# Two products of the last pair of tiles but one are moved into the last pair's order, and one more output goes out whole from ScalarE

## The chip, the cores and the metric

The kernel runs on one core of a Trainium2 chip. The metric is the device time of one execution in microseconds (us). A core has TensorE (matrix products, results in PSUM), VectorE, ScalarE, GpSimd and SyncE, each with its own queue of instructions that it takes in order, and 16 DMA engines that move data between HBM and SBUF. In the profile they are called PE (PEld for its weight loads), DVE, ACT, POOL and SP; a name with a q (SPq, ACTq) is the queue's own work, such as issuing a DMA.

## What is computed

Attention over 8 batches, 12 heads, 448 tokens and 64 columns a head, and behind it a two-layer network on the 3584 tokens with 768 columns, with 2048 columns between the layers:

```python
def _attn_ref(q, k, v):
    scores = np.matmul(q, k.transpose(0, 1, 3, 2)) / np.sqrt(q.shape[-1])
    attn = np.exp(scores - np.max(scores, axis=-1, keepdims=True))
    attn = attn / (np.sum(attn, axis=-1, keepdims=True) + 1e-09)
    return np.matmul(attn, v)

def _moe_ref(x, w_in, w_out):
    h = x @ w_in
    g = h * (1.0 / (1.0 + np.exp(-h)))
    return g @ w_out
```

The change touches the last product alone, `g @ w_out`, at its very end.

## The kernel before, in words

**Tiles and stages.** Scores, exponentials and attention come first, unit by unit; the first layer follows for two batches at a time, and the second layer, `g @ w_out`, mixes in as its inputs come free. In the last 40 us only the second layer runs. Its rows are cut into 28 tiles of 128 tokens, and two neighbouring tiles make a pair, numbered 0 to 13 (`qd` in the code; `LAST` is 13). Each of the two tiles has two halves of 384 output columns, so a pair has four output blocks of 128 x 384, called (0,0), (0,1), (1,0) and (1,1): tile, half.

**Seven products for eight.** A pair computes its four blocks with seven block products in place of eight, in Winograd's manner: each product runs over eight 128-row pieces, so it is eight matmuls of 128 x 384 (L922, L683 within `times`). Products 1, 2, 4 and 7 take rows of G (the activated first layer), products 5, 6 and 3 take rows S that VectorE combines from G beforehand (`combine_g`, L916). Three buffers S exist (`NSG`, L273). On the side of the weights, products 1, 2, 3 and 7 use `w_out_t` and 4, 5 and 6 combined weights D. So the profile's tile names tell the products apart: `w_out_t,G` is 1, 2 or 7, `D,S` is 5 or 6, and `w_out_t,S` is 3.

**Banks and reads.** Products 1, 6, 7 (and 4) add up in one PSUM bank, 5 and 3 in a second, 2 stands alone in a third (`BANK`, L918). Four banks are handed round. After product 1 ScalarE copies the bank to block (0,0), after 5 to (1,1), after 6 to (0,1) (`take_copy`, L1004). Product 6 may begin only when the copy of 1 is done, 7 only when the copy of 6 is done, 3 only when the copy of 5 is done, since each adds to what the copy reads. After 2, 7 and 3 VectorE adds the bank to (0,0), (1,1) and (0,1) and the block is stored (`take_sum`, L1023). In pairs 12 and 13 product 4 is itself replaced by a smaller scheme of seven products over both pairs, run ahead of pair 12 (`FOLD`, `AHEAD_OF`); the block (1,0) is completed and stored after product 7 by `take_last` (L1018). In pair 13, the last, product 2 is cut into two halves of 192 columns that stand at the very end; each is added and stored by `take_end` (L1010, its DMAs in L1014).

**Stores.** `store` (L981, DMA in L997) cuts a block by the batch in which its rows lie: rows of batches other than the last go out in pieces of 32, rows of the last batch in 64 or 128. In pairs 12 and 13 the pieces go in turn to SyncE and ScalarE. Pair 13's block (1,0) goes out whole, from ScalarE (L989, L995); its blocks (1,1) and (0,1) go out as two halves of 64 rows each, one from SyncE and one from ScalarE.

**What sets the order.** The program's order is written out by a planner inside the kernel (`Order`, and the loop at its end). It keeps a list `moe` of pieces of TensorE work with their inputs, and whenever TensorE is free it runs the first piece of the list whose inputs are ready and whose bank is free (`moe_ready`, L1876, over the first 80 pieces); pieces are single matmuls of a product (L1832). `queue_quad` (L1738) puts a pair's products into the list: for pairs before the last in the order 1, 5, 6, 2, 7, 3, 4, for the last 1, 5, 6, 7, 3, 4 and then the two halves of 2 (L1826). The reads and stores of a product are written out by the planner when the product is due to end. The engines then take their queues in order.

Of the kernel before, what the change touches and what calls it, by code (L numbers as in the profile page):

```python
# [29 lines left out]
def mm(n):  # L30
    return n / 2400.0 + 0.0026
# [183 lines left out]
def kernel(  # L215
# [42 lines left out]
    folded = {(q, m) for a, b, ms in FOLD for q in (a, b) for m in ms}  # L258
# [15 lines left out]
    LAST = NT * B // 4 - 1  # L274
# [447 lines left out]
    HF = NFF // 2  # L722
# [199 lines left out]
    def product(qd, m, f0, f1, strips, c0=0, c1=OH):  # L922
        w = {1: rows(2 * qd, 0), 2: rows(2 * qd, 1), 4: rows(2 * qd + 1, 1), 7: rows(2 * qd + 1, 0)}
        w = w[m] if m in w else S_t[(qd, m)]
        if BANK[m] == m and f0 == 0:
            pr_t[(qd, m)] = psum_bank(f"p_{qd}_{m}" + "r" * (c0 > 0))
        if c1 - c0 < OH:
            half_t[c0] = pr_t[(qd, m)]
        for f in range(f0, f1):
            times(  # L930
                pr_t[(qd, BANK[m])][:, 0 : c1 - c0],
                w[:, f, :],
                W_[m][:, f, c0:c1],
                f == 0 and BANK[m] == m,
                f == HF - 1,
                strips,
            )
# [43 lines left out]
    def store(qd, i, j):  # L981
        u, t = divmod(2 * qd + i, NT)
        w, turn = 0, 0
        while w < 4:
            r, col = divmod(128 * t + 32 * w, S)
            b = 2 * u + r
            dst = out[b * S : (b + 1) * S, OH * j : OH * (j + 1)]
            if b == B - 1:
                n = 4 if w == 0 and (qd < LAST or (i, j) == OUT[4]) else 2  # L989
                dst = dst[col : col + 32 * n]  # L990
            else:
                n = 1
                dst = dst.rearrange("(i g) m -> g i m", g=TPP)[col // 32]
            eng = nc.scalar if turn % 2 and 4 * qd + 8 >= NT * B else nc.sync
            if qd == LAST and (i, j) == OUT[4]:  # L995
                eng = nc.scalar
            eng.dma_start(out=dst, in_=ost_t[(qd, i, j)][32 * w : 32 * (w + n), :])  # L997
            w, turn = w + n, turn + 1

    OUT = {1: (0, 0), 5: (1, 1), 6: (0, 1), 4: (1, 0)}  # L1000
    SUM = {2: (0, 0), 7: (1, 1), 3: (0, 1)}
# [6 lines left out]
    def take_end(p, c0, c1):  # L1008
        t = ost_t[(LAST, 0, 0)][:, c0:c1]
        nc.vector.tensor_tensor(out=t, in0=p, in1=t, op=ALU.add)  # L1010
        row = out.shape[0] - 256
        for lo, eng in ((0, nc.sync), (64, nc.scalar)) if c0 else ((0, nc.sync),):
            hi = lo + 64 if c0 else 128
            eng.dma_start(out=out[row + lo : row + hi, c0:c1], in_=t[lo:hi])  # L1014
# [222 lines left out]
    def take_bank(name):  # L1237
        bank_of[name] = m_ring.take()

    def leave_bank(name):  # L1240
        return lambda at: m_ring.give(at, bank_of[name])
# [336 lines left out]
    def sum_read(qd, m, at):  # L1578
        made = sum_reads.setdefault((qd, m), [])
        made.append(at)  # L1580
        if m and len(made) == (1 if m == 3 else 3):
            sg_ring.give(max(made))
# [40 lines left out]
    def plan_folds():  # L1623
# [24 lines left out]
        for i in (1, 2, 3, 4):  # L1648
# [2 lines left out]
                Op("DVE", 0.43, lambda i=i: fold_x(g, m, i, homes[i - 1]), made + more, 1)  # L1651
            )

    fold_done, ahead, ends = [], {}, []

    def queue_fold(g, m):
# [81 lines left out]
    def queue_quad(qd):  # L1738
# [4 lines left out]
        def read(m, deps):  # L1743
            def then(at):
                if m in (2, 3, 4):
                    leave_bank(f"p_{qd}_{BANK[m]}")(at)
                if m in (2, 3, 4, 7) and (qd, m) not in folded:
                    home.give(at + STORE)

            fn, eng = (take_copy, "ACT") if m in OUT else (take_sum, "DVE")  # L1750
            busy = act(OH) if eng == "ACT" else OH / 960.0 + 0.13
            bias = -2 if eng == "ACT" else -4
            took[m] = od.add(Op(eng, busy, lambda: fn(qd, m), deps, bias, then=then))

        def queue(m, f0, f1, c0=0, c1=OH):
            first = {6: (1,), 2: (1,), 7: (6, 5), 3: (5, 6) if qd == LAST else (5, 6, 7), 4: (7,)}.get(m, ())

            def run():
                strips = od.mode == "cols" and bool(qk_seq or av_seq)
                op = Op(  # L1760
                    "PE",
                    (f1 - f0) * mm(c1 - c0),
                    lambda: product(qd, m, f0, f1, strips, c0, c1),
                    tail=PE_OUT,
                )
                if BANK[m] == m and f0 == 0:
                    take_bank(f"p_{qd}_{m}" + "r" * (c0 > 0))
                for ring, need in rings:
                    ring.take(need)
                if m in (5, 6, 3) and f1 == HF:  # L1770
                    op.then = lambda at: sum_read(qd, m, at)
                od.on_pe(op, "cols" if strips else "full", (f1 - f0) * (4 if strips else 1))
                if f1 < HF or c1 < OH:
                    begun[m] = (HF if c0 else 0) + f1
                if f1 < HF:
                    return
                if c1 - c0 < OH:
                    fn = lambda: take_end(half_t[c0][:, 0 : c1 - c0], c0, c1)
                    od.add(Op("DVE", 0.33, fn, [op, took[1]], -4))
                    return  # L1780
                pr_op[(qd, m)] = op
                read(m, [op] + [took[x] for x in {2: (1,), 7: (5,), 3: (6,)}.get(m, ())])
                if m == 7 and (qd, 4) in folded:
                    if qd in ahead:
                        def then(at):
                            leave_bank(f"p_{qd}_1")(at)
                            home.give(at + STORE)

                        od.add(
                            Op(  # L1790
                                "DVE",
                                OH / 960.0 + 0.13,
                                lambda: take_last(qd),
                                [op, took[7], ahead[qd]],
                                -4,
                                then=then,
                            )
                        )
                    else:
                        read(4, [op, took[7]])  # L1800

            def deps():
                if f0 or c0:
                    return [] if begun.get(m) == (HF if c0 else 0) + f0 else [None]
                made = list(w_op.get(m, [None]))
                hard = {6: (1,), 7: (6,), 3: (5,), 4: (7,)}.get(m, ())
                made += [took.get(x) if x in hard else (took.get(x), 9.0) for x in first]
                if m in (1, 2, 4):
                    t = 2 * qd + m // 4
                    i = int(m != 1)  # L1810
                    for f in range(HF):
                        made += [(y, f * mm(OH)) for y in gates_at(t, f + HF * i)]
                    return made + ld_wout
                x = sg_op.get((qd, m), [None, None])
                return made + [x[0], (x[1], 4 * mm(OH))]

            rings = ((home, 1),) if f0 == 0 and (m in OUT or m == 7 and (qd, 4) in folded and qd not in ahead) else ()
            moe.append((deps, int(BANK[m] == m and f0 == 0), run, rings))


        begun = {}
        took_of[qd] = took
        for g, k in AHEAD_OF:
            if min(FOLD[g][:2]) - LEAD == qd:
                queue_fold(g, k)
        for m in (1, 5, 6, 2, 7, 3, 4) if qd < LAST else (1, 5, 6, 7, 3, 4):  # L1826
            if m == (3 if TAIL and qd == LAST else 4):
                for g, (a, b, ms) in enumerate(FOLD):
                    for k in ms if max(a, b) == qd else ():
                        if (g, k) not in AHEAD_OF:  # L1830
                            queue_fold(g, k)
            for f0 in range(0, HF, 1):  # L1832
                if (qd, m) not in folded:
                    queue(m, f0, f0 + 1)
        if qd == LAST and TAIL:
            ends.pop()()
        elif qd == LAST:
            for c in range(2):
                for f0 in range(0, HF, 1):
                    queue(2, f0, f0 + 1, OH // 2 * c, OH // 2 * (c + 1))  # L1840
# [347 lines left out]
    while True:  # L2188
# [45 lines left out]
        m = m_ring.when(1)  # L2234
        dark = m is None or m > od.now
        if warm["on"] and not dark and od.free["PE"] <= od.now and wait > QUIET and od.now > 0.9:
            each = mm(128) if od.now > COLD else 0.107
            n = max(1, int((wait - 0.06) / each), int(wait / each + 0.9) * (od.now < COLD))
            wide = 4
            if warm.pop("first", None):  # L2240
                n, wide = FIRST, 4
# [36 lines left out]
```

## Time and profile before

| | |
|---|---|
| time, median of 3 runs | 380.45 us (380.25 to 380.97) |
| the profiled execution | 379.91 us |
| its span in the profile | 378.1 us |
| granted TensorE clock | 0.999 |
| VectorE, ScalarE, GpSimd busy | 75%, 68%, 22% of the span |
| read from HBM, written | 45.61 MB, 11.01 MB |

The span runs from the first to the last instruction that the profiler saw; the execution's own time has 1.8 us more around it. A row of the timeline gives start, duration, engine, line, operation, tiles, shapes and count; what stands in brackets is the idle time before it and what ended that. A matmul's end is modelled and lies past the start of the next one, since matmuls overlap. A row for a DMA on SPq or ACTq is the time that the queue takes to issue it; its data move later, and the landing is told in the view of the DMAs. A row of the windows gives the stretch and its length, then busy time and count for PE, PEld, DVE, ACT and POOL, the granted clock, the DMA share and GB/s.

### The profile page before, as it was taken

The page shows a single profiled execution, that of the slowest core. Times are in us where ns is not written, and L with a number is a line of the kernel's source. Part 1 is how long each engine was busy: PE and PEld are TensorE (multiplying, and loading weights), DVE is VectorE, ACT ScalarE, POOL GpSimd, SP SyncE. Part 2 cuts the span into 40 slices and gives each one's busy share as a digit, 9 for nine tenths or more (in the row PEclk, how much of TensorE's full clock was granted, in tenths as well). Part 3 has the DMA queues.
Part 4 walks back from the last instruction along what each step waited for, and adds up shares of the span by engine and source line. Part 5 has one row for each costly group of instructions (what it writes and reads, how often), then busy time and mean ns, then how long its engine had stood idle before and what let it go on. Part 6 is the DMA issues. An engine that isn't in the chain of part 4 may idle for free.

```text
span 378.1 us, 9953 instructions
## 1 busy us (share of the span) xinstructions
PE 371.4 (98%) x4018; PEld 187.4 (50%) x4018; DVE 284.0 (75%) x588; ACT 255.7 (68%) x401; POOL 85.0 (22%) x155
## 2 busy tenths in 40 slices
PE   8999999999999999999999999999999999999994
PEld 3365445444544444444444444445556655556763
DVE  3667959999995969995969998897575334489852
ACT  4988873897877797868788778558872248873210
POOL 6652438433026316006423200000000000000000
PEclk9999999999999999999999999999999999999999
DMA  7999999928149849048955421200002330001343
GB/s 118 199 207 210 207 203 177 195 29 121 19 101 152 146 50 138 12 105 114 179 67 74 53 53 33 69 17 0 2 2 68 85 96 5 0 0 44 85 127 83
DMA packets 35982, 34.47 MB, mean 91 GB/s; under 512 B 11872, under 2 KB 35168, under 8 KB 35936
## 3 DMA queue, kind: packets, MB, share of 16 engines
q0 software_dynamic: 25312, 22.82, 40.7%
q1 hardware_dynamic: 10144, 10.48, 10.3%
q8 instruction: 31, 0.51, 0.5%
q10 hardware_dynamic: 480, 0.54, 0.4%
q14 instruction: 15, 0.12, 0.1%
HBM read 45.61 MB, written 11.01 MB: 150 GB/s over the span
## 4 chain that ended last, share of the span: by engine, by line
PE 96%; DMA 1%; ACT 1%; DVE 1%; issue 0%; DVEq 0%; POOLq 0%
PE p L683 29%; PE h L683 21%; PE f L683 16%; PE s L446 12%; PE a L568 8%; PE o L683 3%; PE a L554 2%; PE a L601 2%; PE n_Q L683 1%; DMA rk<-in_k_dram 1%; PE n_P L683 1%; ACT T L491 1%; PE z L2180 0%; PE z L683 0%; DVE ost L1023 0%
## 5 line engine op out<-in xcount | busy, mean ns | idle before, releaser
L502 ACT ACTIVATE E<-s 128x896 f16<-128x896 f32 x164 | 141.9, 922 | 24.7 <-PE s L446 24.6
L683 PE MATMUL h<-xT,w_in_t 128*32 128x448 f16 (+2 forms) x762 | 83.6, 348 | 0.0
L683 PEld LDWEIGHTS <-w_in_t 128*128 128x128 f16 (+1 forms) x909 | 54.5, 97 | 50.1 <-issue 8.1
L352 POOL DMA_DIRECT2D V<-in_v_dram x88 | 48.4, 561 | 48.8 <-PE a L568 29.2
L683 PEld LDWEIGHTS <-G 128*128 128x128 f16 (+1 forms) x672 | 42.5, 97 | 29.7 <-issue 5.0
L715 ACT ACTIVATE th<-h 128x448 f16<-128x448 f32 x67 | 36.6, 546 | 24.2 <-PE h L683 21.0
L683 PE MATMUL p<-w_out_t,G 128*128 128x384 f16 (+2 forms) x326 | 50.9, 324 | 0.0
L446 PE MATMUL s<-rq,KT 32*128 32x448 f16 (+3 forms) x728 | 45.4, 347 | 0.6 <-DVE rq L410 0.3
L1004 ACT COPY ost<-p 128x384 f32<-128x384 f32 x42 | 20.1, 480 | 31.8 <-PE p L683 20.6
L683 PEld LDWEIGHTS <-S 128*128 128x128 f16 (+1 forms) x321 | 29.5, 98 | 22.1 <-issue 3.4
L759 DVE SCALAR_TENSOR_TENSOR G<-th,h 128x448 f16<-128x448 f16 (+1 forms) x64 | 35.7, 573 | 4.7 <-ACT th L715 4.3
L683 PE MATMUL p<-D,S 128*128 128x384 f16 (+1 forms) x217 | 38.8, 326 | 0.0
L1023 DVE TENSOR_TENSOR ost<-p,ost 128x384 f32<-128x384 f32 x31 | 17.1, 552 | 23.7 <-ACT ost L1004 12.6
L568 PE MATMUL a<-E,V 128*32 128x448 f16 (+1 forms) x640 | 32.7, 356 | 0.0
L332 POOL DMA_DIRECT2D rq<-in_q_dram x25 | 14.0, 560 | 68.9 <-PE s L446 59.8
L671 DVE SCALAR_TENSOR_TENSOR xT<-a,rdn 128x448 f16<-128x448 f32 x46 | 26.9, 618 | 2.9 <-PE a L568 2.2
L446 PEld LDWEIGHTS <-KT 32*128 32x128 f16 (+1 forms) x824 | 12.5, 96 | 31.0 <-issue 29.7
L515 DVE TENSOR_TENSOR T<-T,E 128x1792 f16<-128x1792 f16 x21 | 22.8, 1086 | 4.5 <-ACT E L502 4.4
L515 DVE TENSOR_TENSOR T<-E,E 128x1792 f16<-128x1792 f16 x21 | 22.7, 1083 | 4.1 <-ACT E L502 4.0
L886 DVE TENSOR_TENSOR p<-f,p 128x448 f32<-128x448 f32 x15 | 9.3, 623 | 19.2 <-PE f L683 11.5
L683 PE MATMUL f<-sx,tw 128*128 128x448 f16 x102 | 23.4, 352 | 0.0
L568 PEld LDWEIGHTS <-V 128*32 128x32 f16 (+1 forms) x640 | 13.5, 95 | 18.1 <-issue 10.5
(128 smaller groups left out, 455.9 us busy)
## 6 DMA issues: line engine op xcount, KB each, us to landing
out_dram<-ost SPq DMA_DIRECT2D x163, 48.0 KB, 1.8
rk<-in_k_dram POOLq DMA_DIRECT2D x24, 224.0 KB, 5.5
rq<-in_q_dram POOLq DMA_DIRECT2D x23, 224.0 KB, 5.8
w_out_t<-in_moe_w_out_dram POOLq DMA_DIRECT2D x4, 768.0 KB, 12.5
V<-in_v_dram POOLq DMA_DIRECT2D x42, 64.0 KB, 4.3
V<-in_v_dram POOLq DMA_DIRECT2D x42, 48.0 KB, 4.7
w_in_t<-in_moe_w_in_dram POOLq DMA_DIRECT2D x6, 256.0 KB, 9.3
w_in_t<-in_moe_w_in_dram POOLq DMA_DIRECT2D x3, 512.0 KB, 12.0
```

The lines of the kernel that those rows point to most:

```text
L332: nc.gpsimd.dma_start(out=rawq[n][:, cols], in_=group_of(q, b, hg)[:, cols])
L352: nc.gpsimd.dma_start(out=VT[b][32 * x : 32 * (x + 1), hs, at : at + count, :], in_=v[b, hs].rearrange("h (i g) d -> i h g d", g=TPP)[:, : ...
L446: nc.tensor.matmul(out=pS[p0 : p0 + 32 * (x1 - x0), h % 2, at : at + q1 - q0], lhsT=KT[(b, hg)][32 * h : 32 * (h + 1), key_rows(b, hg, c, ...
L502: nc.scalar.activation(out=E[(n, w)][:, 2 * y : 2 * y + 2, :], in_=pS_t[(n, w, y)][:, :, 0:S], func=AF.Exp, scale=attn_scale,)
L515: nc.vector.tensor_tensor(out=T[n], in0=T[n] if step else E[(n, 0)], in1=E[(n, step + 1)], op=ALU.add,)
L568: nc.tensor.matmul(out=a[32 * h : 32 * (h + 1), 0:S], lhsT=VT[b][k0:k1, HG * hg + h, place(b, hg, c), part - 1 :: 2], rhs=e[k0:k1, h], sta ...
L671: nc.vector.scalar_tensor_tensor(out=x3(b, cc)[:, cc % 3, 32 * g0 : 32 * g1], in0=acc[(n, part)][:, 0:nq], scalar=0.5, in1=rdn_t[n].rearra ...
L683: nc.tensor.matmul(out=out[i : i + cut], lhsT=w[:, i : i + cut], rhs=x, start=start, stop=stop, skip_group_check=True,)
L715: nc.scalar.activation(out=th, in_=h_t[(b, f, t0)][:, 0:n], func=AF.Tanh)
L759: nc.vector.scalar_tensor_tensor(out=dst[:, f, at + lo : at + hi], in0=th_t[(b, f, t0)][:, lo - t0 : hi - t0], scalar=1.0, in1=h_t[(b, f, ...
L1004: nc.scalar.copy(out=ost(qd, *OUT[m]), in_=bank(qd, BANK[m]))
L1023: nc.vector.tensor_tensor(out=t, in0=bank(qd, BANK[m]), in1=t, op=ALU.add)
```

## The change

Pair 12 no longer puts its products 3 and 2 into the list. It leaves its `queue` function in `kept`, and pair 13 calls it: all eight matmuls of 12's product 3 stand behind 13's product 6, and all eight of 12's product 2 behind 13's product 7. The list is then 1, 5, 6, 7 for pair 12, and for pair 13: 1, 5, 6, (12's 3), 7, (12's 2), 3, and the two halves of 2. What each product computes, reads and stores stays as it is. Besides, pair 13's block (0,1), `SUM[3]`, is stored as one DMA of 128 rows from ScalarE in place of 64 rows from SyncE and 64 from ScalarE.

```diff
@@ -986,13 +986,13 @@
             b = 2 * u + r
             dst = out[b * S : (b + 1) * S, OH * j : OH * (j + 1)]
             if b == B - 1:
-                n = 4 if w == 0 and (qd < LAST or (i, j) == OUT[4]) else 2
+                n = 4 if w == 0 and (qd < LAST or (i, j) in (OUT[4], SUM[3])) else 2
                 dst = dst[col : col + 32 * n]
             else:
                 n = 1
                 dst = dst.rearrange("(i g) m -> g i m", g=TPP)[col // 32]
             eng = nc.scalar if turn % 2 and 4 * qd + 8 >= NT * B else nc.sync
-            if qd == LAST and (i, j) == OUT[4]:
+            if qd == LAST and (i, j) in (OUT[4], SUM[3]):
                 eng = nc.scalar
             eng.dma_start(out=dst, in_=ost_t[(qd, i, j)][32 * w : 32 * (w + n), :])
             w, turn = w + n, turn + 1
@@ -1651,6 +1651,7 @@
+    kept = []
     fold_done, ahead, ends = [], {}, []
...
@@ -1819,6 +1820,7 @@
         begun = {}
+        left_over, kept[:] = (kept or [None])[0], [queue]
         took_of[qd] = took
...
@@ -1830,8 +1832,11 @@
             for f0 in range(0, HF, 1):
-                if (qd, m) not in folded:
+                if (qd, m) not in folded and not (qd == LAST - 1 and m in (3, 2)):
                     queue(m, f0, f0 + 1)
+            for k, at in ((3, 6), (2, 7)) if qd == LAST else ():
+                for f0 in range(0, HF * (m == at), 1):
+                    left_over(k, f0, f0 + 1)
```

## The prediction

> **What bounds the kernel now.** I read the page first: which engine is busy, and which chain ended last.
>
> ```profile
> span 378.1 us, 9953 instructions
> PE 371.4 (98%) x4018; PEld 187.4 (50%) x4018; DVE 284.0 (75%) x588; ACT 255.7 (68%) x401; POOL 85.0 (22%) x155
> PE 96%; DMA 1%; ACT 1%; DVE 1%; issue 0%; DVEq 0%; POOLq 0%
> ```
>
> TensorE is busy for 98% of the span and is 96% of the chain that ended last. The change takes no matmul away and adds none, so it can gain only where TensorE waits, or after its last matmul. Next, TensorE's timeline from the place where the moved products stand. Columns: start, duration, line, tiles, count.
>
> ```profile
> 361.11 3.09 PE L683 MATMUL p<-w_out_t,G 128*128 128x384 f16 x18
> 364.04 1.46 PE L683 MATMUL p<-w_out_t,S 128*128 128x384 f16 x8
> 365.34 1.14 PE L683 MATMUL p<-w_out_t,G 128*128 128x384 f16 x6
> 366.31 2.76 PE L683 MATMUL p<-D,S 128*128 128x384 f16 x16
> 368.91 0.41 PE L683 MATMUL p<-w_out_t,G 128*128 128x192 f16 x3
> 369.16 0.81 PE L683 MATMUL p<-w_out_t,S 128*128 128x384 f16 x4
> 369.81 1.46 PE L683 MATMUL p<-w_out_t,G 128*128 128x384 f16 x8
> 371.11 0.81 PE L683 MATMUL p<-w_out_t,S 128*128 128x384 f16 x4
> 371.76 0.58 PE L683 MATMUL p<-w_out_t,G 128*128 128x192 f16 x5
> 372.17 0.82 PE L683 MATMUL p_2r<-w_out_t,G 128*128 128x192 f16 x8
> ```
>
> I write 12.2 for product 2 of pair 12. By the operands, the 18 are 12.2, 12.7 and two of 13.1; then come 12.3, the other six of 13.1, 13.5 and 13.6, three of 13.2's first half, half of 13.3, 13.7, the rest of 13.3, and 13.2. From 364.04 to 365.34 eight matmuls take 1.30 us, 0.1625 each, and every row starts where the one before leaves off: TensorE waits nowhere. Its last matmul ends at 372.17 + 0.82 = 372.99. The span ends at 378.1, so 5.1 us lie behind it. VectorE's and the DMA issues' timelines show what fills them:
>
> ```profile
> 371.38 0.56 DVE L1023 TENSOR_TENSOR ost<-p,ost 128x384 f32<-128x384 f32 x1 [4.56 <-PE p L683]
> 371.86 0.55 DVE L1018 TENSOR_TENSOR ost<-p,ost 128x384 f32<-128x384 f32 x1
> 372.32 0.55 DVE L1023 TENSOR_TENSOR ost<-p,ost 128x384 f32<-128x384 f32 x1
> 372.78 0.35 DVE L1010 TENSOR_TENSOR ost<-p,ost 128x192 f32<-128x192 f32 x1
> 373.05 0.34 DVE L1010 TENSOR_TENSOR ost<-p_2r,ost 128x192 f32<-128x192 f32 x1
> ```
>
> ```profile
> 371.97 0.47 SPq L997 DMA_DIRECT2D out_dram<-ost  x1
> 371.97 0.54 ACTq L997 DMA_DIRECT2D out_dram<-ost  x1
> 372.60 0.76 ACTq L997 DMA_DIRECT2D out_dram<-ost  x1
> 372.89 0.47 SPq L997 DMA_DIRECT2D out_dram<-ost  x1
> 373.46 0.65 ACTq L997 DMA_DIRECT2D out_dram<-ost  x1
> 373.46 0.54 SPq L1014 DMA_DIRECT2D out_dram<-ost  x1
> 374.09 0.55 SPq L1014 DMA_DIRECT2D out_dram<-ost  x1
> 374.23 0.54 ACTq L1014 DMA_DIRECT2D out_dram<-ost  x1
> ```
>
> The last sum is done at 373.05 + 0.34 = 373.39, yet its two stores (L1014, the last two rows) are issued only at 374.09 and 374.23: SyncE is still issuing the store before it, and ScalarE is still issuing 13.3's second half (373.46 + 0.65 = 374.11). So eight stores crowd behind one product that ended late (13.7, at 369.81 + 1.46 = 371.27). Then the transfers, as issue to landing and as rate:
>
> ```profile
> out_dram<-ost ACTq DMA_DIRECT2D x1, 48.0 KB, 2.9
> out_dram<-ost SPq DMA_DIRECT2D x2, 192.0 KB, 2.0
> out_dram<-ost SPq DMA_DIRECT2D x6, 48.0 KB, 1.8
> out_dram<-ost ACTq DMA_DIRECT2D x3, 48.0 KB, 2.0
> ```
>
> ```profile
> 371.00:373.00 2.00, 2.00 (x19) 1.44 (x17) 1.62 (x4) 0.00 (x0) 0.00 (x0) 1.00 0.00 0
> 373.00:375.00 2.00, 0.00 (x0) 0.00 (x0) 0.39 (x2) 0.00 (x0) 0.00 (x0) 1.00 0.80 187
> 375.00:376.00 1.00, 0.00 (x0) 0.00 (x0) 0.00 (x0) 0.00 (x0) 0.00 (x0) 1.00 1.00 326
> ```
>
> The first row is the very last store: 374.23 + 2.9 = 377.1. The next three are medians from 360 us on: the same sizes land in 1.8 to 2.0 us where little else is under way. The last columns of the windows are DMA share and GB/s: nothing moves until 373, one microsecond after the first of these issues, and at 375 to 376 the DMA engines are fully busy. The last store is late twice: issued 0.84 us after its data, and 0.9 to 1.1 us longer under way because 768 KB go out together. From 377.1 to 378.1 the program closes.
>
> **The change, part by part.** *TensorE.* The planner runs the first product in its list whose inputs are ready. 12.7 adds onto 12.6's bank and so waits for ScalarE's copy of it. That gap was filled by 12.2; now 13.1, next in the list, must fill it.
>
> ```profile
> 361.31 0.48 ACT L1004 COPY ost<-p 128x384 f32<-128x384 f32 x1 [1.65 <-PE p L683]
> 342.36 0.48 ACT L1004 COPY wide<-p 128x384 f32<-128x384 f32 x1 [0.82 <-PE p L683]
> ```
>
> ```profile
> 342.16 0.81 PE L683 MATMUL p<-w_out_t,G 128*128 128x384 f16 x4
> 342.81 0.33 PE L683 MATMUL p<-D,S 128*128 128x384 f16 x1
> 342.97 1.46 PE L683 MATMUL p<-w_out_t,G 128*128 128x384 f16 x8
> ```
>
> The copy ends at 361.79. Pair 10 shows the same gap filled by five matmuls of the next pair (4 + 1 rows): copy done at 342.84, 10.7 starts at 342.97, with no wait. Five of 13.1 from 361.11 bring 12.7 to 361.92, the same 0.13 us behind its copy. Cost 0; bounds 0 to 0.16 (one more matmul's width). It needs a free PSUM bank: 12.1 and 12.5 hold two of four, 13.1 and 13.5 take the others. 12.5's bank stays held until 12.3, but 12.2 comes only after 12.7's sums have freed a bank. From there: rest of 13.1 to 363.71, 13.5 to 365.01, 13.6 to 366.31, then 12.3 (fills the wait for 13.6's copy, which three and four matmuls of 13.2 and 13.3 filled before) to 367.61, 13.7 to 368.91, 12.2 to 370.21, 13.3 to 371.51, and 13.2's halves. The sum is unchanged: last matmul at 372.99.
>
> *VectorE.* 13.3 needs its combined operand S, two operations of about 0.4 us, in one of three S buffers. 13.5's comes free at 365.01; at worst it is 12.3's, at 367.61, plus 0.1 and 0.75: 368.5, and 13.3 starts at 370.21. Cost 0, with 1.7 us of cover. Sums start 0.11 us after a product's end (371.27 to 371.38 above). So 13.7's sum and the one behind it (L1018) run near 369.2 to 370.2 instead of 371.4 to 372.4, 12.2's at 370.5 and 13.3's at 371.8 to 372.3 (before 372.32 to 372.87). The last is bound by TensorE before and after: 373.05 to 373.39.
>
> *Stores.* 13.7's two and the whole one of L1018 leave at 369.8 to 371.2. 12.2's is three issues (two SyncE, one ScalarE) at 371.1 to 372.0. 13.3's is one whole issue by ScalarE at 372.40, 0.76 by the 192 KB row, done at 373.16; SyncE loses one issue. 13.2's first half is summed at 372.44 to 372.79 and issued by SyncE at 372.86 to 373.40. Both queues are then free, and the last two stores go out at 373.46 to 373.50 (0.07 to 0.11 behind their sum; the first issues above, at 371.97, stand 0.03 behind theirs). **Gain at the issue: 374.23 - 373.48 = 0.75 us.**
>
> *Transfers.* Bounds for the last store: 2.9 us (as now) and 1.8 (the free row). Behind the ScalarE issue at 372.40 now stand 192 + 96 + 48 + 48 = 384 KB instead of 768 KB from 371.97. Moving from 373.4 at 187 to 326 GB/s, 393 kB take 1.2 to 2.1 us, so to 374.6 to 375.5, plus landing. I take 2.25 us, nearest the 2.0 row with some crowding left: it lands at 375.7. **Second gain 0.65 us.** [...]
>
> **Sum.** 377.1 - 1.4 = 375.7, plus 1.0 of closing: span 376.7. The profiled execution took 379.91, 1.8 around its span, and lies 0.54 under the median of 380.45; taken off the median, 1.35 (I keep 0.05 for the gap at 12.7) gives **379.1**. This kernel's measurement can tell 0.2%, 0.76 us, from no change.
>
> **Rivals.** *The transfers stay as slow.* The last store still needs 2.9 us, because 12.2's 192 KB, new in the tail, go out just ahead. 373.48 + 2.9 = 376.4: gain 0.75, **379.7**. For it: all L1014 stores took about 2.9. Against: half the bytes.
>
> *The issues exclude each other.* If SyncE and ScalarE can't issue at once, the order after 372.40 is 0.76 + 0.54 + 0.55 + 0.54, with the last issue starting near 374.25, as now; only the shorter transfer is left, and part of that: gain 0.35, **380.1**. Against: SyncE's 0.47 at 372.89 lies inside ScalarE's 0.76 from 372.60 and is no longer than at 371.97. The Trainium skill, Perfetto Trace Analysis, section DMA Instruction — HWDGE, says that an issue locks the descriptor generator for exclusive use; these overlapping rows show no such wait between two queues.
>
> *Slower: ScalarE's queue in order.* Now 12.3's sum and store belong to the stretch where 13.6's copy is due. If ScalarE's part of that store stood ahead of the copy, ScalarE would wait for 12.3 (ends 367.77 with its drain), 0.1, the S operations at 0.75, the sum at 0.56, and 0.4 to issue: 369.6, then 0.48 of copy and 0.1, and 13.7 starts at 370.2 instead of 367.61. TensorE, in order too, stands 2.6 us; less 1.35 gained, **381.7**. It decides as soon as the store is ahead of the copy, and is slower from 1.35 us of standing on. For it, the trace has such a case: ScalarE's store at 366.18 ends 0.05 before 13.1's copy.
>
> ```profile
> 366.18 0.37 ACTq L997 DMA_DIRECT2D out_dram<-ost  x1
> 366.60 0.48 ACT L1004 COPY ost<-p 128x384 f32<-128x384 f32 x1 [4.80 <-DVE S L916]
> ```
>
> Against: 13.6 ends a whole product (1.30 us) before 12.3, and the planner writes each out when its input is due.
>
> *The change doesn't do what it says.* The list is only a preference; with another pick the two products end up where they were, and **380.45** stays.
>
> **Chances.** Forecast, 378.6 to 379.5: 0.65. Transfers as slow, 379.7: 0.15, half of it over the 0.2%. Issues exclusive, 380.1: 0.07. ScalarE's order, 381.7: 0.07. No effect: 0.06, a third of it slower by some unseen wait. Faster 0.65 + 0.07 = 0.72; slower 0.07 + 0.02 = 0.09; same 0.19. The range 378.6 to 380.2 holds the first three cases, 0.87, less a little at the low end.
>
> **What would show it.** Right: TensorE without a gap from 361 us on and the same end, near 373.0; 13.7 ending near 369; six VectorE operations spread from 369 on; the L1014 stores of the last half starting together near 373.5, ScalarE's issue before them 0.76 long and over by 373.2; the last landing 2.0 to 2.5 us after issue. Wrong: a gap ahead of 12.7 or 13.7, a ScalarE copy late behind a store, or a last landing still 2.9 us after its issue.

## The result, and the profile after

| | before | after |
|---|---|---|
| time, median of 6 runs each | 380.19 us (379.92 to 380.97) | 378.70 us (378.33 to 379.11) |
| ratio | | 0.9959, 95% interval 0.9946 to 0.9972 |
| span of the profiled execution | 378.1 us | 376.7 us |

The kernel became 1.5 us faster, to 378.7 us; 379.1 was forecast. The page of the kernel after, its first lines and its chain:

```profile
span 376.7 us, 9950 instructions
PE 370.6 (98%) x4018; PEld 187.2 (50%) x4018; DVE 284.5 (76%) x588; ACT 255.6 (68%) x401; POOL 85.0 (23%) x155
PE 95%; DVE 1%; ACT 1%; DMA 1%; issue 0%; DVEq 0%; POOLq 0%
```

The same 4018 matmuls, and TensorE still makes up the chain. Its timeline after, from 12.6's end on:

```profile
361.26 2.76 PE L683 MATMUL p<-w_out_t,G 128*128 128x384 f16 x16
363.86 2.76 PE L683 MATMUL p<-D,S 128*128 128x384 f16 x16
366.46 1.46 PE L683 MATMUL p<-w_out_t,S 128*128 128x384 f16 x8
367.76 2.76 PE L683 MATMUL p<-w_out_t,G 128*128 128x384 f16 x16
370.36 1.46 PE L683 MATMUL p<-w_out_t,S 128*128 128x384 f16 x8
371.66 0.82 PE L683 MATMUL p<-w_out_t,G 128*128 128x192 f16 x8
372.32 0.82 PE L683 MATMUL p_2r<-w_out_t,G 128*128 128x192 f16 x8
```

In order: 13.1 with 12.7 in its midst (16), 13.5 and 13.6, 12.3, 13.7 and 12.2, 13.3, the two halves of 13.2, with no gap. TensorE ends at 373.14, against 373.00 before; this end moves by up to 1.9 us between the executions profiled here, so the kernels are compared from it on. VectorE and the last issues, after:

```profile
365.36 0.76 DVE L916 TENSOR_TENSOR S<-G,S 128x512 f16<-128x512 f16 x2 [0.77 <-PE p L683]
369.33 0.56 DVE L1023 TENSOR_TENSOR ost<-p,ost 128x384 f32<-128x384 f32 x1 [0.76 <-PE p L683]
372.52 0.36 DVE L1010 TENSOR_TENSOR ost<-p,ost 128x192 f32<-128x192 f32 x1
373.18 0.36 DVE L1010 TENSOR_TENSOR ost<-p_2r,ost 128x192 f32<-128x192 f32 x1 [0.30 <-PE p_2r L683]
```

```profile
370.55 0.74 ACTq L997 DMA_DIRECT2D out_dram<-ost  x1
372.52 0.35 ACTq L997 DMA_DIRECT2D out_dram<-ost  x1
373.56 0.47 SPq L1014 DMA_DIRECT2D out_dram<-ost  x1
373.61 0.49 ACTq L1014 DMA_DIRECT2D out_dram<-ost  x1
```

13.7's sum starts at 369.33 in place of 371.38. The last sum ends at 373.54, and both of its stores are issued at once. The view of the DMAs, for these two stores, with the time from issue to landing last:

```profile
out_dram<-ost SPq DMA_DIRECT2D x1, 48.0 KB, 1.8
out_dram<-ost ACTq DMA_DIRECT2D x1, 48.0 KB, 2.1
```

373.61 + 2.1 = 375.7 is the last landing, and the program closes 1.0 us later. So the tail behind TensorE went from 5.14 to 3.59 us, in two parts: the last store is issued 0.47 us behind TensorE's end in place of 1.23, and is 2.1 us under way in place of 2.9.

### The profile page after: what moved, and what is told of

It is laid out like the page before. It is cut to its first block, busy times and chain, and to the rows that moved or that the text cites. A ratio compares the mean times of both kernels' runs of the same rounds, so it can differ in the third digit from the quotient of the medians.

```text
span 376.7 us, 9950 instructions
## 1 busy us (share of the span) xinstructions
PE 370.6 (98%) x4018; PEld 187.2 (50%) x4018; DVE 284.5 (76%) x588; ACT 255.6 (68%) x401; POOL 85.0 (23%) x155
## 4 chain that ended last, share of the span: by engine, by line
PE 95%; DVE 1%; ACT 1%; DMA 1%; issue 0%; DVEq 0%; POOLq 0%
PE p L683 30%; PE h L683 21%; PE f L683 16%; PE s L446 11%; PE a L568 8%; PE o L683 3%; PE a L554 2%; PE a L601 2%; PE n_Q L683 1%; DMA rk<-in_k_dram 1%; ACT T L491 1%; PE n_P L683 1%; PE z L683 0%; PE z L2185 0%; PE z L554 0%
## 5 line engine op out<-in xcount | busy, mean ns | idle before, releaser
L568 PEld LDWEIGHTS <-V 128*32 128x32 f16 (+1 forms) x640 | 13.5, 95 | 18.1 <-issue 10.1
```

The lines of the kernel that those rows point to most:

```text
L568: nc.tensor.matmul(out=a[32 * h : 32 * (h + 1), 0:S], lhsT=VT[b][k0:k1, HG * hg + h, place(b, hg, c), part - 1 :: 2], rhs=e[k0:k1, h], sta ...
```

## The experiments

All kernels side by side; every column is read off the kernel's own profile (us), the ratio is to the kernel before on the same chip, with its interval.

| kernel | time | ratio | TensorE's end to last issue | issue to landing | TensorE's end to the span's end |
|---|---|---|---|---|---|
| before | 380.19 | 1 | 1.23 | 2.92 | 5.14 |
| after | 378.70 | 0.9959 (0.9946 to 0.9972) | 0.47 | 2.08 | 3.59 |
| e1, whole store alone | 379.97 | 0.9991 (0.9981 to 1.0000) | 1.00 | 2.51 | 4.55 |
| e2, move alone | 378.84 | 0.9960 (0.9946 to 0.9975) | 0.56 | 2.10 | 3.58 |
| e3, few bytes | 379.18 | 0.9970 (0.9958 to 0.9981) | 1.23 | 2.00 | 4.21 |
| e4, free queue | 382.36 | 1.0051 (1.0035 to 1.0067) | 0.48 | 2.78 | 7.40 |
| e5, 12.3 moved alone | 378.43 | 0.9960 (0.9947 to 0.9972) | 0.47 | 2.08 | 3.59 |
| e6, 12.2 moved alone | 379.39 | 0.9980 (0.9970 to 0.9991) | 0.47 | 2.39 | 3.90 |
| e7, 13.7 late | 379.24 | 0.9975 (0.9964 to 0.9987) | 0.82 | 2.35 | 4.20 |
| e8, cut at 256 | 378.54 | 0.9963 (0.9951 to 0.9975) | 0.53 | 1.99 | 3.50 |
| e9, five issues | 378.85 | 0.9958 (0.9942 to 0.9973) | 0.47 | 2.06 | 3.63 |
| e10, one last issue | 378.14 | 0.9944 (0.9925 to 0.9964) | 0.42 | 1.64 | 3.10 |
| e11, one last, cut at 256 | 378.19 | 0.9946 (0.9926 to 0.9966) | 0.53 | 1.61 | 3.18 |
| e12, halved by columns | 378.62 | 0.9954 (0.9941 to 0.9968) | 0.83 | 2.02 | 3.76 |

My theory at first was this: eight stores crowd behind a 13.7 that ends late, and the crowd costs twice, in issue and, by its 768 KB, in transfer. Rivals: the one or the other alone, or a gain of TensorE's order as such.

**e1 and e2: the two parts of the change apart.** e1 is the kernel before with the two edits in `store`; e2 is the kernel after without them.

```diff
-                n = 4 if w == 0 and (qd < LAST or (i, j) == OUT[4]) else 2
+                n = 4 if w == 0 and (qd < LAST or (i, j) in (OUT[4], SUM[3])) else 2
...
-            if qd == LAST and (i, j) == OUT[4]:
+            if qd == LAST and (i, j) in (OUT[4], SUM[3]):
```

> Only the whole store of block (0,1) from ScalarE, no product moved. Theory (the end is set by when the last store can be issued and by how many bytes stand ahead of it): no gain, 380.2 within 0.3, because ScalarE still issues three stores ahead of its last one and the bytes stay. Rival (the store itself brings much of it): 379.3 or less.

> Only the two products moved; block (0,1) goes out in two halves as before. Theory: all of the gain, 378.7 within 0.3, since 13.3's halves leave both queues about 0.6 us before the last sum is done. Rival (the whole store is needed): 379.3 or more.

e2 has the whole gain, so with the products moved the whole store adds nothing that can be told. e1 was a miss in part: I expected nothing, and its tail is 0.59 us shorter, of which the ratio shows 0.34 us, with an interval that reaches 1. The crowd was one issue smaller, but its bytes were the same and still landed faster. My account had no reason for that.

**e3 and e4: issue and transfer apart.** In e3 the last pair's three blocks store 128 of 384 columns, and the rest of them stays unwritten. In e4 GpSimd takes block (0,1) whole, and the very last store goes out whole from ScalarE.

```diff
+            m = 128 if qd == LAST else OH
-            eng.dma_start(out=dst, in_=ost_t[(qd, i, j)][32 * w : 32 * (w + n), :])
+            eng.dma_start(out=dst[:, 0:m], in_=ost_t[(qd, i, j)][32 * w : 32 * (w + n), 0:m])
```

```diff
-                n = 4 if w == 0 and (qd < LAST or (i, j) == OUT[4]) else 2
+                n = 4 if w == 0 and (qd < LAST or (i, j) in (OUT[4], SUM[3])) else 2
...
+            if qd == LAST and (i, j) == SUM[3]:
+                eng = nc.gpsimd
...
-        for lo, eng in ((0, nc.sync), (64, nc.scalar)) if c0 else ((0, nc.sync),):
-            hi = lo + 64 if c0 else 128
+        for lo, eng in ((0, nc.scalar if c0 else nc.sync),):
+            hi = 128
```

> The kernel before, but the last pair's three blocks (1,1), (1,0) and (0,1) store only their first 128 of 384 columns (the rest of these blocks is left unwritten): as many issues as before, 384 KB in the tail in place of 768. Theory (two terms, issue 0.75 and transfer 0.8): only the transfer term goes, span 377.3 to 377.5, time about 379.5; last stores still issued near 374.1. Rival A (the issue is all): 380.2. Rival B (the bytes are all): 378.7.

> The kernel before with all bytes, but block (0,1) is issued whole by GpSimd, and the last half's store whole by ScalarE, so that ScalarE's queue is free when the last sum is done. Theory: only the issue term goes, last issue near 373.5, landing 2.6 to 3.1 us later, span 377.2 to 377.6, time about 379.5. Rival A (the issue is all): 378.7. Rival B (the bytes are all): 380.2. If GpSimd's own store lands last, the run tells nothing of this.

In e3 the issues are as late as before, and with 384 KB in place of 768 the landing is back at 2.0 us: the terms do come apart. Its ScalarE issues, of which the second is a whole block cut to 64 KB:

```profile
372.47 0.55 ACTq L998 DMA_DIRECT2D out_dram<-ost  x1
373.11 0.74 ACTq L998 DMA_DIRECT2D out_dram<-ost  x1
374.73 0.53 ACTq L1015 DMA_DIRECT2D out_dram<-ost  x1
```

These take 0.55 and 0.74 us with a third of the bytes, as they did with all (0.54 and 0.76). So the length of an issue isn't set by its bytes. The last row is the last store, still 1.23 us behind TensorE's end. e4's profile shows the other term alone, as expected: the last issue comes 0.48 us behind TensorE's end, and its landing still takes 2.78. Its time tells nothing of that: the stores have all landed 3.26 us behind TensorE's end, 0.89 sooner than before, but then GpSimd's queue closes. The line of its closing instructions, with shortest, median and longest in ns, and first and last start in us:

```profile
L2275 POOLq DRAIN  x3: 46/102/6468, 373.0 to 380.0; - x3
```

The long one begins with GpSimd's store at 373.0 and holds the program's end until 379.5.

**e5, e6, e7: which move, and where 13.7 must stand.** Against the kernel after:

```diff
 e5
-                if (qd, m) not in folded and not (qd == LAST - 1 and m in (3, 2)):
+                if (qd, m) not in folded and not (qd == LAST - 1 and m == 3):
-            for k, at in ((3, 6), (2, 7)) if qd == LAST else ():
+            for k, at in ((3, 6),) if qd == LAST else ():
 e6: the same with m == 2 and ((2, 7),)
 e7
-        for m in (1, 5, 6, 2, 7, 3, 4) if qd < LAST else (1, 5, 6, 7, 3, 4):
+        for m in (1, 5, 6, 2, 7, 3, 4) if qd < LAST else (1, 5, 6, 3, 7, 4):
-            for k, at in ((3, 6), (2, 7)) if qd == LAST else ():
+            for k, at in ((3, 6), (2, 6)) if qd == LAST else ():
```

> Only 12.3 is moved (behind 13.6); 12.2 stays in pair 12, where it fills the wait ahead of 12.7; the whole store stays. Theory (what counts is that 13.7 and its two blocks are done early): 13.7 ends 2.6 us before TensorE's end in place of 3.9, still early enough, 378.7 within 0.3. Rival (each moved product brings its share): 379.3 to 379.6.

> Only 12.2 is moved (behind 13.7; it then also fills the wait ahead of 13.7); 12.3 stays in pair 12; the whole store stays. Theory: 13.7 ends 3.1 us before TensorE's end, 378.7 within 0.3. Rival (each moved product brings its share): 379.3 to 379.6.

> Both products are moved, but both stand behind 13.6 and 13.7 comes after 13.3, 1.3 us before TensorE's end. The whole store stays. Theory: the sums and stores of 13.7 and of the block behind it crowd again at the end: 576 KB from about 372.5 and last issue near 373.9: 379.4 to 379.9. Rival (moving the products is what helps, wherever 13.7 stands): 378.7.

e5 has the whole gain with 12.3 alone. e7, with both moved but 13.7 late, has some 60% of it by the tail (0.94 of 1.55 us). So it isn't the moving as such: what counts is how long before the end 13.7 is done. e6 fell short, and its TensorE and ScalarE timelines show one cause:

```profile
366.46 1.46 PE L683 MATMUL p<-D,S 128*128 128x384 f16 x8 [0.19 <-ACT ost L1004]
```

```profile
365.49 0.40 ACTq L997 DMA_DIRECT2D out_dram<-ost  x1
365.93 0.86 ACT L1004 COPY ost<-p 128x384 f32<-128x384 f32 x2 [4.34 <-DVE S L916]
```

ScalarE's part of 12.3's store, at 365.49, stands ahead of its copy of 13.1; 13.6 waits for that copy and TensorE stands 0.19 us. The tail is 0.31 longer as well. Together that is 0.5 us. The times differ by 0.7 to 1.0 from those of the kernel after and e5; what the rest is stays open, since the one profile is that of the shortest of its runs.

**e8, e10, e11: what is left of the tail.** e8 cuts product 2 of the last pair at column 256; e10 is the kernel after with the very last store in one issue; e11 has both.

```diff
 e8
-            for c in range(2):
+            for c0, c1 in ((0, 256), (256, OH)):
                 for f0 in range(0, HF, 1):
-                    queue(2, f0, f0 + 1, OH // 2 * c, OH // 2 * (c + 1))
+                    queue(2, f0, f0 + 1, c0, c1)
 e10
-        for lo, eng in ((0, nc.sync), (64, nc.scalar)) if c0 else ((0, nc.sync),):
-            hi = lo + 64 if c0 else 128
+        for lo, eng in ((0, nc.sync),):
+            hi = 128
```

> The changed kernel with product 2 of the last pair cut into 256 and 128 columns in place of 192 and 192. Theory: what is left behind TensorE is one sum, one issue and one transfer, each a little shorter for 128 columns: 0.05 to 0.15 us less, 378.6, not to be told from 378.7 by time, but by the last sum's 0.29 in place of 0.36 us. Rival: matmuls of 128 columns run at the pace of their weight loads, and TensorE ends later by up to 0.2 us: 378.9.

> The changed kernel with its very last store as one issue of 128 rows from SyncE in place of 64 rows from each of SyncE and ScalarE. Theory: ScalarE's half is issued 0.05 us later than SyncE's and lands 0.3 later; one issue from SyncE lands 1.9 us after it like the half before it: TensorE's end to the span's end 3.3 to 3.4 us in place of 3.6, time 378.4. Rival (128 rows on one queue take longer than 64 on each of two): 378.9.

> As e10_one_last, with product 2 cut into 256 and 128 columns as well. Theory: both small gains add up, 3.2 to 3.3 us behind TensorE, 378.3; not to be told from e10 by time. Rival: as for e10, 378.8.

e8 does what was expected of it, 0.09 us in the tail, and nothing that the time can tell. Its rival falls: from 13.3's start TensorE takes 2.78 us to its end, as in the kernel after. e10 did more than expected: one issue of 128 rows, 96 KB, lands in 1.6 us, while two of 64 rows, 48 KB each, took 1.8 and 2.1. It has the shortest tail, 3.10 us, and the lowest time, 378.14; its interval overlaps that of the kernel after, so only the profile says that it beats it. e11 adds nothing to it: the first half's store is later there, and the last one waits behind it. e10 was the second sign, after e1, that the stores of 64 rows are the slow ones.

**e9 and e12: no product moved, all bytes kept.** e9 has five whole issues in place of eight. e12 keeps eight, from the same queues, and cuts blocks (1,1) and (0,1) by columns in place of rows.

```diff
 e9
-                n = 4 if w == 0 and (qd < LAST or (i, j) == OUT[4]) else 2
+                n = 4 if w == 0 else 2
-            if qd == LAST and (i, j) == OUT[4]:
-                eng = nc.scalar
+            if qd == LAST:
+                eng = nc.scalar if (i, j) == OUT[4] else nc.sync
-        for lo, eng in ((0, nc.sync), (64, nc.scalar)) if c0 else ((0, nc.sync),):
-            hi = lo + 64 if c0 else 128
+        for lo, eng in ((0, nc.sync if c0 else nc.scalar),):
+            hi = 128
 e12
-                n = 4 if w == 0 and (qd < LAST or (i, j) == OUT[4]) else 2
+                n = 4 if w == 0 else 2
-            eng.dma_start(out=dst, in_=ost_t[(qd, i, j)][32 * w : 32 * (w + n), :])
+            for c in (0, OH // 2) if qd == LAST and (i, j) != OUT[4] else (None,):
+                h = slice(0, OH) if c is None else slice(c, c + OH // 2)
+                e = eng if c is None else nc.scalar if c else nc.sync
+                e.dma_start(out=dst[:, h], in_=ost_t[(qd, i, j)][32 * w : 32 * (w + n), h])
```

> The kernel before, no product moved and all bytes kept, but the last pair's tail goes out in five issues in place of eight: block (1,1) whole by SyncE, (1,0) whole by ScalarE, (0,1) whole by SyncE, the first half of product 2 by ScalarE, the last half whole by SyncE; GpSimd issues none. Theory: the issue term goes, the last store is issued about 0.5 us after TensorE's end in place of 1.2 and still needs 2.6 to 2.9 us: TensorE's end to the span's end 4.2 to 4.4 us in place of 5.1, time 379.2 to 379.5. Rival (the bytes are all): 380.1. Rival (the issues are all): 378.6.

> The kernel before, no product moved, the same eight issues from the same queues with the same bytes, but the two blocks (1,1) and (0,1) are halved by columns (128 rows of 192 columns each) in place of by rows (64 rows of 384 columns); the last half's store stays in two of 64 rows. Theory now (stores of 64 rows are slow to issue, slow down what follows them, and move at half the rate): issues of 0.35 us in place of 0.47 to 0.76, last issue about 0.5 us after TensorE's end, landing near 2.1 us, 3.6 to 3.8 us behind TensorE, time 378.7 to 378.9. Rival (the number of issues and their crowd is what costs): 1.2 and 2.9 us as before, 380.1.

Both have the whole gain of the change, with 13.7 as late as before and all 768 KB behind it. For e9 that was a miss: I expected its last landing to take 2.6 to 2.9 us, and it took 2.1. e9's windows and the landings of its five stores:

```profile
373.00:374.00 1.00, 0.03 (x1) 0.00 (x0) 0.43 (x2) 0.00 (x0) 0.00 (x0) 1.00 1.01 363
374.00:375.00 1.00, 0.00 (x0) 0.00 (x0) 0.00 (x0) 0.00 (x0) 0.00 (x0) 1.00 1.01 336
```

```profile
out_dram<-ost SPq DMA_DIRECT2D x2, 192.0 KB, 2.0
out_dram<-ost ACTq DMA_DIRECT2D x1, 192.0 KB, 2.0
out_dram<-ost ACTq DMA_DIRECT2D x1, 96.0 KB, 2.0
out_dram<-ost SPq DMA_DIRECT2D x1, 96.0 KB, 2.1
```

363 and 336 GB/s, where the kernel before has these in the same two microseconds:

```profile
373.00:374.00 1.00, 0.00 (x0) 0.00 (x0) 0.39 (x2) 0.00 (x0) 0.00 (x0) 1.00 0.73 197
374.00:375.00 1.00, 0.00 (x0) 0.00 (x0) 0.00 (x0) 0.00 (x0) 0.00 (x0) 1.00 0.86 178
```

In these two microseconds the bytes move at nearly twice the rate. e9 has fewer issues too, so it can't tell number from form; e12 can. Its issues of full height, and its windows:

```profile
372.13 0.34 SPq L1000 DMA_DIRECT2D out_dram<-ost  x1
372.13 0.38 ACTq L1000 DMA_DIRECT2D out_dram<-ost  x1
372.61 0.39 ACTq L1000 DMA_DIRECT2D out_dram<-ost  x1
373.06 0.33 SPq L1000 DMA_DIRECT2D out_dram<-ost  x1
373.09 0.41 ACTq L1000 DMA_DIRECT2D out_dram<-ost  x1
```

```profile
373.00:374.00 1.00, 0.16 (x2) 0.00 (x0) 0.56 (x3) 0.00 (x0) 0.00 (x0) 1.00 0.99 337
374.00:375.00 1.00, 0.00 (x0) 0.00 (x0) 0.00 (x0) 0.00 (x0) 0.00 (x0) 1.00 0.95 320
```

There are eight issues as before, but these five took 0.33 to 0.41 us where the halves by rows took 0.47 to 0.65 and the whole store behind one 0.76, and 337 and 320 GB/s were moved. The first two stores of the tail, issued together with nothing else under way, landed after 2.2 and 2.4 us by rows and after 1.8 and 2.0 by columns. The last issue came 0.83 us behind TensorE's end, and not 0.5 as expected. The theory that the number of stores and their bytes alone make the crowd falls with this run. What holds: **in this tail, halves of 64 rows are slow to issue, slow down what is issued right behind them, and take longer to land**, and before, two pairs of them stood right ahead of the last store. One such pair need not cost: in e2, 13.3's halves are issued at 373.60, 0.6 us ahead of TensorE's end, and the tail is as short as that of the kernel after.

It isn't both halves that move slowly. The view of the DMAs gives packets, MB and share of the 16 engines for each queue, here for the kernel before (over 6.5 us) and then for e12 (over 5.4 us). By the MB, q1 is SyncE's queue and q10 ScalarE's:

```profile
q1 hardware_dynamic: 384, 0.34, 24.9%
q10 hardware_dynamic: 384, 0.44, 19.4%
```

```profile
q10 hardware_dynamic: 512, 0.44, 25.8%
q1 hardware_dynamic: 512, 0.34, 19.5%
```

SyncE's 0.34 MB kept the engines busy for 24.9% of 6.5 us before, which is 1.62 us, and for 1.05 us in e12; ScalarE's 0.44 MB took 1.26 and 1.39 us. So only SyncE's bytes were slower by rows. The rest of the lower rate is engines that stood idle: their busy share in the two microseconds was 0.73 and 0.86 before, against 0.99 and 0.95 in e12.

## Why the prediction was right, and where it was not

- **TensorE**: right to the matmul. Five of 13.1 cover 12.6's copy, and no gap shows from 361 us on.
- **VectorE**: right. 13.3's operand took 13.5's buffer (365.36, behind 13.5's end), and the last sum ends 0.4 us behind TensorE in both kernels.
- **Issue**, 0.75 forecast: the last issue came 0.76 nearer to TensorE's end. The whole store of 13.3 took 0.35 and not 0.76: the row of 0.76 that I took the price from was one behind a 64-row store (as 370.55 after, 0.74), and no price of a whole store. It made no difference here: 0.76 too would have been over before the last sum.
- **Transfers**, 0.65 forecast: 0.84 measured. The size was near, but this is the step whose reason was only half right. It held that the last store is 0.9 to 1.1 us longer under way "because 768 KB go out together". In e9 and e12 the 768 KB go out together and land 1.8 to 2.2 us after issue, so the bytes alone don't do it. In halves by rows they do count: e3 keeps that form with 384 KB, and its last store lands after 2.0 us. The moves took 13.7's halves out of the last microseconds and 384 KB with them, and e7 gained less because there they came late again. No run tells how much of the moves' gain is the form and how much the bytes.
- **Luck**: the span came out at 376.7, just as forecast. The tail shrank by 1.55 us and not by 1.4, and TensorE happened to end 0.14 us later in this execution.
- **The transfers stay as slow**: no. **The issues exclude each other**: no. In e12, SyncE and ScalarE issue from 372.13 on together, in 0.34 and 0.38 us; apart from each other, in e9, such issues took 0.33 to 0.35 and 0.36. The exclusive lock of the descriptor generator that the Trainium skill describes (Perfetto Trace Analysis, DMA Instruction — HWDGE) shows no wait of an issue's length there.
- **ScalarE's queue in order**: not in this change, but the mechanism is real; e6 shows it at the copy of 13.1, with 0.19 us of standing and not 2.6.
- **A rule that I didn't weigh**: the Trainium skill, DMA: Bandwidth & Descriptors, Rules for kernel authors, says of two transfers to disjoint halves of the partitions that they serialize, since they share the same DMA engines, and advises one transfer of 128 partitions. e9 and e10 agree with the advice. That halves by rows also move less in the same time, 178 to 197 against 320 to 363 GB/s in e9 and e12, is what the runs add.

What stays open is why halves of 64 rows are slow, and whether SyncE's bytes are slow for their queue or for their rows. For the issue it isn't that fewer rows take longer: in the kernel before, from 300 us on, most stores of 32 rows were issued in 0.31 to 0.43 us.

## What to carry to other kernels

Where a kernel ends with stores, compare the issue time and the landing time of the last ones with those of other stores of the same size in the same trace: a store that is slow in the tail may be slow for its form, and then the form is the thing to change before any work is moved. Here a block of 128 rows was better cut by columns than by rows, or not cut. An order of work that gives the gain isn't proof of its reason: here a few lines in the cut of two blocks' stores gave the same.

## What the runs showed of the hardware that I had not expected

- Issue times, in all these runs from 300 us on: 128 rows took 0.33 to 0.46 us where no 64-row store was just ahead, 64 rows 0.47 to 0.66, and 128 rows right behind 64 rows 0.73 to 0.78 on ScalarE and 0.47 to 0.54 on SyncE. A third of the bytes (e3) changed nothing in this.
- As the last of all, one store of 128 rows landed 1.6 us after issue, with 96 KB in e10 and 64 KB in e11, sooner than the two halves of 48 KB in the kernel after (1.8 and 2.1).
- A store by GpSimd at the end costs its queue's drain of 6.5 us (e4); the same drain stands in the kernel before with 6.66 us, but in the middle of the span, where it hides.
